# Clustered attention and a gated FFN on one core: one sum, one reciprocal and one product for the two heads of a pair in the first batch, with a new table of places

## Chip, cores and metric

The kernel runs on one core of a Trainium2 chip. The metric is the time of the device for one execution in microseconds (us). The engines are named as in the profile: PE (TensorE, matrix products; PEld is its weight load), ACT (ScalarE), DVE (VectorE), POOL (GpSimd) and SP (SyncE, which issues most DMAs).

## The reference

Attention in which a query sees only the keys of its own cluster, followed by a gated FFN. There are 4 batches, 8 heads, 768 positions and 64 dimensions for a head.

```python
q_assign = argmax(einsum('bhsd,hcd->bhsc', q_n, c_n))      # q_n, k_n, c_n: normalised; 16 clusters for a head
k_assign = argmax(einsum('bhsd,hcd->bhsc', k_n, c_n))
mask = q_assign[:, :, :, None] == k_assign[:, :, None, :]
scores = where(mask, (1 / 8) * q @ k.T, -1e9)
attn = softmax(scores) ; a = attn @ v                      # x: 3072 tokens x 512, heads side by side
gate = sigmoid(x @ w_gate) ; val = x @ w_val               # 512 -> 1536
out = (gate * val) @ w_out                                 # 1536 -> 512
```

## The kernel before

The work of a batch is cut into *steps*. One step takes 128 keys of one head and the queries of a half of the sequence (3 chunks of 128): PE makes the scores (`sc`, line 652), ACT takes the exponential into `es` (line 657), and three steps later PE multiplies `es` by the head's v with a column of ones beside it (`av`, line 675), so that the weighted sum and the sum of weights gather in one PSUM tile. In batch 0 all four pairs of heads are run half by half: steps 0 to 47 are the first half of the queries of heads 0 to 7 (six steps for a head, so head 7 begins at step 42), steps 48 to 95 the second half.

The mask is part of the product. Before a head's first step its k and q are split into two float16 parts: a high half (`hi`, a cast, line 873) and a low half (`lo`, the difference, line 880), laid side by side in `hl`. PE transposes `hl` into PSUM (`tu`, `t_ps`, line 901), and an engine copies that to `T` (`ev`, lines 912 and 914). PE multiplies `T` by the centroids (`lg`, line 390), DVE takes the maximum and compares (`pk`, lines 929 and 937), PE transposes the result (`ot`, `oh_ps`, line 961), and it is placed in rows 64 to 79 of `T` (`pl0` for k, line 982; `pl1` for q, line 986): two positions of different clusters then get a large negative score. The second half of a pair's queries, "the rest" (`r0` to `r3`, lines 997 to 1056), goes the same way later.

When a head's six steps are done, `normalise` (lines 335 to 347) adds to `av` a tiny multiple of the sum of v (`sv`), takes the reciprocal of the sum of weights, both on DVE (lines 339 and 341), and multiplies on POOL into one half of the pair's tile `xp` (line 344). After the pair's second head `xp` is transposed into `xT`, by PE (`x_ps`, line 703) and a copy (line 704) or by a DMA. The FFN of half a batch needs all four pairs of that half: `g` (line 477) and `v` (line 497) are its two first products, `o` (line 517) the last. They are put into a queue from which every step takes a few.

The order on each engine is written out by a table, `SCHED`. A place such as `"h4lo0": 5.0` says that this piece (head 4, low half, side 0 = k) is issued behind step 5; `r0hi` is the high half of pair 0's rest, `vc` the cast of v, `w` the weight loads, `b1p2tn0` a piece of batch 1, pair 2. Keys that end in `E` choose the engine (`A` ACT, `D` DVE, `P` POOL); without one, `hi`, `ev` and places are DVE's and `lo` POOL's. The engines run their queues in order, each as fast as its waits allow: places fix the order, not the time. `nd7` would put dummy products ahead of step 7's scores. The branch that the table now switches on is in the program already:

```python
both = nq == 3 and b < SCHED.get("pn", 0)
...
elif e == 1:
    normalise2(av, nq, b, p, x)
```

Of the kernel before, what the change touches and what calls it, by code (L numbers as in the profile page):

```python
# [19 lines left out]
]  # L20
SCHED = {
# [70 lines left out]
}  # L92


# [1254 lines left out]
```

## Time and profile before

| | |
|---|---|
| time, median of 3 runs | 327.67 us (327.52 to 328.28) |
| the profiled execution | 328.03 us, of which the span from the first to the last instruction is 325.9 us |
| granted TensorE clock | 1.000 |
| busy, share of the span | PE 98%, PEld 64%, DVE 59%, ACT 72%, POOL 33% |
| first score, first gate product | 9.09 us, 40.37 us |
| HBM | 28.34 MB read, 6.29 MB written |

A row of the timeline gives start, duration, engine, line, operation and output<-input, with the idle time before it and what ended it in brackets. A row of a group gives shapes, the count, the busy time, the mean duration of one in ns, and the idle time before them. Matmul records overlap: the distance from one start to the next is shorter than a record.

### The profile page before, as it was taken

What the parts mean: (1) busy time and instruction counts of PE and PEld (TensorE: products, weight loads), DVE (VectorE), ACT (ScalarE), POOL (GpSimd) and SP (SyncE); (2) the same over time, 40 slices, a digit from 0 to 9 for tenths busy, and PEclk for the clock granted to TensorE, in tenths of its full rate; (3) what the DMA queues carried; (4) which work ended last, traced back from release to release, by engine and by line L of the source; (5) the groups of instructions that cost most, each with busy time, mean ns of one, the idle gap of its engine ahead of it and who ended that gap; (6) DMA issues with size and microseconds to landing.
All of it is one profiled execution on the core that took longest, in us unless ns stands there. A gap on an engine that the chain in (4) does not pass through costs nothing.

```text
span 325.9 us, 8840 instructions
## 1 busy us (share of the span) xinstructions
PE 319.4 (98%) x3363; PEld 207.7 (64%) x3363; DVE 190.7 (59%) x527; ACT 234.8 (72%) x527; POOL 108.4 (33%) x150
## 2 busy tenths in 40 slices
PE   7999999999999999999999999999999999999996
PEld 5878766766766666666566655666566655654654
DVE  5899858877767666657546655667544322441431
ACT  6697998777899988877677777887778877332420
POOL 5876554143435365334232443323210111000000
PEclk9999999999999999999999999999999999999999
DMA  6999996719896995963897473932731012102002
GB/s 190 360 263 188 266 157 116 208 28 203 230 221 174 152 260 128 275 180 76 159 196 172 135 98 103 252 82 53 139 91 37 2 24 78 44 2 94 3 2 97
DMA packets 77994, 45.14 MB, mean 139 GB/s; under 512 B 56896, under 2 KB 75008, under 8 KB 77952
## 3 DMA queue, kind: packets, MB, share of 16 engines
q1 hardware_dynamic: 73984, 39.73, 51.5%
q0 software_dynamic: 3680, 4.72, 8.7%
q8 instruction: 26, 0.43, 0.5%
q14 instruction: 16, 0.13, 0.1%
q10 hardware_dynamic: 288, 0.13, 0.1%
HBM read 28.34 MB, written 6.29 MB: 106 GB/s over the span
## 4 chain that ended last, share of the span: by engine, by line
PE 92%; DVE 3%; DMA 2%; ACT 1%; POOL 1%; issue 1%; ACTq 0%; DVEq 0%
PE g L477 19%; PE v L497 19%; PE o L517 18%; PE sc L652 18%; PE av L675 10%; PE lg L403 2%; DMA kraw<-in_k_dram 2%; PE o_end L549 1%; PE lg L390 1%; PE t_ps L901 1%; PE wm L743 1%; DVE T L982 1%; PE oh_ps L961 1%; POOL hl L880 0%; PE t_ps L784 0%
## 5 line engine op out<-in xcount | busy, mean ns | idle before, releaser
L657 ACT ACTIVATE es<-sc 128x384 f16<-128x384 f32 x384 | 175.1, 493 | 42.6 <-PE sc L652 37.2
L652 PE MATMUL sc<-T 128*128 128x384 f16 x384 | 117.9, 326 | 0.7 <-DVE T L986 0.4
L675 PEld LDWEIGHTS <-es 128*128 128x128 f16 x1152 | 81.5, 98 | 49.1 <-ACT es L657 0.2
L675 PE MATMUL av<-va,es 128*128 128x65 f16 x1152 | 97.6, 194 | 0.0
L504 DVE SCALAR_TENSOR_TENSOR hT<-th,v 128x384 f16<-128x384 f32 x96 | 53.2, 554 | 67.1 <-PE av L675 44.7
L497 PE MATMUL v<-xTb,wv 128*128 128x384 f16 x384 | 78.1, 326 | 0.0
L477 PE MATMUL g<-xTb,wg 128*128 128x384 f16 x384 | 78.0, 326 | 0.0
L517 PE MATMUL o<-wo,hT 128*128 128x512 f16 x276 | 75.1, 379 | 0.0
L344 POOL TENSOR_TENSOR xp<-t,rec 128x192 f16<-128x192 f32 (+1 forms) x46 | 29.6, 643 | 126.9 <-DVE rec L341 76.1
L485 ACT ACTIVATE th<-g 128x384 f32<-128x384 f32 x96 | 47.2, 492 | 25.6 <-DVE hT L504 17.9
L477 PEld LDWEIGHTS <-wg 128*128 128x128 f16 x384 | 37.2, 97 | 20.4
L497 PEld LDWEIGHTS <-wv 128*128 128x128 f16 x384 | 37.4, 98 | 19.9
L652 PEld LDWEIGHTS <-T 128*128 128x128 f16 x384 | 37.1, 97 | 1.1 <-DVE T L986 1.1
L517 PEld LDWEIGHTS <-hT 128*128 128x128 f16 x276 | 26.7, 97 | 16.2
L339 DVE TENSOR_TENSOR t<-av,sv 128x195 f32<-128x195 f32 (+1 forms) x46 | 20.1, 437 | 24.4 <-PE av L675 20.8
L1215 POOL TENSOR_TENSOR hl<-kraw,hl 128x384 f16<-128x384 f32 x22 | 20.7, 945 | 24.3 <-issue 13.6
L1215 POOL TENSOR_TENSOR hl<-qraw,hl 128x384 f16<-128x384 f32 x22 | 21.6, 983 | 12.2 <-DVE hl L1214 11.2
L418 DVE TENSOR_REDUCE lgs<-lg 128x192 f32<-128x384 f32 x23 | 12.7, 551 | 11.4 <-PE lg L403 11.3
L526 ACT ACTIVATE ob<-o 128x512 f32<-128x512 f32 x15 | 8.9, 595 | 10.8 <-PE o L517 10.7
L291 POOL CAST va<-vraw 128x768 f16<-128x768 f32 x16 | 13.5, 842 | 2.5 <-DMA vraw<-in_v_dram 2.5
L524 DVE TENSOR_SCALAR ob<-o 128x512 f32<-128x512 f32 x8 | 5.5, 691 | 13.6 <-PE o L517 13.4
L403 PE MATMUL lg<-cm,T 128*128 128x32 f16 x288 | 11.1, 176 | 0.0
(115 smaller groups left out, 232.3 us busy)
## 6 DMA issues: line engine op xcount, KB each, us to landing
vraw<-in_v_dram SPq DMA_DIRECT2D x16, 384.0 KB, 5.5
out_dram<-ob SPq DMA_DIRECT2D x23, 256.0 KB, 2.2
kraw<-in_k_dram SPq DMA_DIRECT2D x15, 384.0 KB, 5.1
qraw<-in_q_dram SPq DMA_DIRECT2D x12, 384.0 KB, 4.9
wg<-in_moe_w_gate_dram POOLq DMA_DIRECT2D x2, 768.0 KB, 9.2
wv<-in_moe_w_val_dram POOLq DMA_DIRECT2D x2, 768.0 KB, 8.9
wo<-in_moe_w_out_dram POOLq DMA_DIRECT2D x2, 768.0 KB, 8.8
qraw<-in_q_dram SPq DMA_DIRECT2D x7, 192.0 KB, 6.7
```

The source lines that it names most:

```text
L339: DVE.tensor_tensor(t[:, 0:nq, :], av, sv, ALU.add)
L344: (eng or POOL).tensor_tensor(x, t[:, 0:nq, 0:64], bcast(rec[:, 0:nq], 64), ALU.mult)
L403: PE.matmul(out=lg[:, bass.ts(i, 32)], lhsT=t[:, c, :], rhs=cm[:, h].rearrange("p s n -> p (s n)"), start=True, stop=True,)
L477: PE.matmul(out=g[:, 0:n], lhsT=wg[fc // WQ][:, dc, fc % WQ, :], rhs=xT[:, dc, t0 : t0 + n], start=(dc == 0), stop=(dc == NDC - 1),)
L485: ACT.activation(th[:, 0:n], g[:, 0:n], AF.Tanh, scale=0.5)
L497: PE.matmul(out=w[:, 0:n], lhsT=wv[fc // WQ][:, dc, fc % WQ, :], rhs=xT[:, dc, t0 : t0 + n], start=(dc == 0), stop=(dc == NDC - 1),)
L504: DVE.scalar_tensor_tensor(hT[:, fc, 0:n], st[1][:, 0:n], 1.0, w[:, 0:n], ALU.add, ALU.mult)
L517: PE.matmul(out=o, lhsT=hT[:, fc, bass.ts(t, 128)], rhs=wo[fc // WON][:, fc % WON, :], start=(fc == 0), stop=(fc == NFC - 1),)
L652: PE.matmul(out=sc.rearrange("p (c t) -> p c t", t=128), lhsT=s["k"], rhs=s["q"], start=True, stop=True,)
L657: ACT.activation(es, sc, AF.Exp, scale=SCALE)
L675: PE.matmul(out=av[:, a0 + s["c0"] + i, :], lhsT=s["es"][:, bass.ts(i, 128)], rhs=VA[b, p][:, e, s["j"], :], start=(first and i == 0 and a ...
L1215: POOL.tensor_tensor(hl[:, :, 64:128], r, hl[:, :, 0:64], ALU.subtract)
```

## The change

The key `pn` is set to 1. For batch 0 (in both halves, since each takes three chunks) the two heads of a pair now share one PSUM tile of 6 x 65 columns; nothing is normalised behind the first head, and behind the second head `normalise2` does the addition, the reciprocal and the product for both. On DVE that is 16 instructions fewer in the program (465 to 449), on POOL 8 products fewer. Apart from this, the table is redone: some 130 places move, most by half a step or one step; a few pieces change engine; three dummy products of 128 columns are put ahead of steps 7, 8 and 46; the loads of batch 0 are issued in another order; and the sum of v of the last pair uses another PSUM pool. Several new keys (`lq`, `lp`, `cd`, `tx`) are read nowhere in this program. The core of the diff, by keys:

```diff
+"pn": 1
-"h4hi0": 1.0, "h4lo0": 5.0, "h5lo0": 8.5, "h6lo0": 23.5
+"h4hi0": 2.0, "h4lo0": 4.5, "h5lo0": 7.5, "h6lo0": 20.5
-"h3lg": 10.5, "h3pk": 11.0, "h4pl0": 20.0, "h4pl1": 22.0, "h7pl0": 40.0, "h7pl1": 40.5
+"h3lg": 9.0, "h3pk": 10.0, "h4pl0": 21.5, "h4pl1": 20.5, "h7pl0": 40.0, "h7pl1": 39.5
-"r0hiE": "A", "h4ev1E": "A", "h5ev1E": "A"            (now DVE)
-"h6lo1E": "D", "r3loE": "D"                           (now POOL)
+"h7hi0E": "P", "r0ev1E": "A", "g0pl1E": "A"           (were DVE)
-"w00": 2.5, "r1tu": 46.5, "r1ot": 54.5, "lag01": 5.5
+"w00": 4.5, "r1tu": 45.5, "r1ot": 53.5, "lag01": 4.5
+"nd7": 1, "nd8": 1, "nd46": 1
-loads of batch 0:  v0 k1 q1 v1 k2 q2 v2 k3 q3 v3
+loads of batch 0:  v0 k1 q1 k2 q2 v1 v2 q3 k3 v3
+"vso33": 1
```

```python
def normalise2(av, nq, b, p, x):
    t = tmpp.tile([128, NCH, 65], FP, name="t")
    sv = SV[b, p].unsqueeze(2).to_broadcast([128, 2, nq, 65])
    DVE.tensor_tensor(t (2, nq, 65), av (2, nq, 65), sv, ALU.add)
    rec = smp.tile([128, NCH], FP, name="rec")
    DVE.reciprocal(rec, t[:, :, 64:65])
    POOL.tensor_tensor(x (nq, 2, 64), t[:, :, 0:64], bcast(rec, 64), ALU.mult)
```

133 rows, old and new, of the table SCHED are left out of this document.

## The prediction

> **What bounds the kernel now.** I read the busy time by stretches first, then the chain of waits, then the waits of the stretch in which PE is not full.
>
> ```profile
> 10.00:20.00 10.00, 9.41 (x172) 7.78 (x169) 8.50 (x28) 8.06 (x20) 9.14 (x15) 1.00 1.09 343
> 20.00:30.00 10.00, 9.48 (x179) 7.78 (x177) 9.54 (x30) 8.11 (x22) 7.38 (x12) 1.00 1.09 188
> 30.00:40.00 10.00, 9.62 (x177) 7.73 (x174) 8.36 (x29) 9.01 (x25) 5.38 (x9) 1.00 1.09 263
> 40.00:50.00 10.00, 10.00 (x106) 6.71 (x103) 5.79 (x16) 8.98 (x23) 5.79 (x9) 1.00 0.98 166
> ...
> 280.00:300.00 20.00, 20.00 (x113) 10.89 (x112) 6.17 (x11) 5.63 (x12) 0.00 (x0) 1.00 0.07 27
> ```
>
> The columns behind the length are PE, PEld, DVE, ACT, POOL, the clock, DMA share and GB/s. From 40 us on PE is busy in the whole of every stretch (the last row shows a late one); before that it is not, and there DVE (9.54 of 10 us between 20 and 30) and POOL (9.14 between 10 and 20) are as full as PE. Busy PE time overstates PE, because the records of consecutive matmuls overlap. The chain of waits shows the true pace:
>
> ```profile
> 40.53 0.65 PE g L477 x4
> ...
> 291.53 7.77 PE o L517 x36
> ```
>
> Four matmuls of 384 columns take 0.65 us (0.16 each, where one record lasts 0.33), and 36 of 512 columns 7.77 us (0.216 each). From the first gate product at 40.4 us to the end PE is a single queue of such work, which the edit neither adds to nor takes from. So the whole effect must come from when this queue starts, which is decided before 40 us. How much is there to win? The waits between 9 and 42 us (waiter, releaser, us in total, times, longest):
>
> ```profile
> PEld L901 <- POOL hl L880: 1.2, 3, 0.5
> PEld L652 <- DVE T L986: 1.1, 3, 0.5
> ...
> PEld L961 <- issue: 0.4, 2, 0.2
> PEld L703 <- POOL xp L344: 0.2, 1, 0.2
> ```
>
> The weight load stands ahead of its matmul and is short, so its waits are PE's real pauses: 1.2 us for the low halves that POOL subtracts, 1.1 for the last place that DVE writes into a head's T, 0.4 + 0.2 for smaller ones. Together 2.9 us: more than this cannot be won without changing the lead-in, whose orders are the same in both programs up to the third score. The largest single pause, with the load's engine, and what follows it on ACT:
>
> ```profile
> 34.30 0.36 DVE L986 TENSOR_SCALAR T<-oh_ps 16x384 f16<-16x384 f16 x1
> 34.72 0.34 PE L652 MATMUL sc<-T 128*128 128x384 f16 x1 [0.38 <-DVE T L986]
> ...
> 35.09 6.24 ACT L657 ACTIVATE es<-sc 128x384 f16<-128x384 f32 x16 [0.31 <-PE sc L652]
> ```
>
> Step 42, the first of head 7, starts when DVE has placed its mask rows (34.66). After it ACT runs 16 exponentials without a pause, 0.39 us each, up to 41.33. So an earlier place of head 7 moves the start of those 16, and with it the gate product, by as much.
>
> **The joint normalisation.** It holds for both halves of batch 0, since every pair there runs three chunks at a time: eight pairs, of which three (pairs 0 to 2) end before step 42.
>
> ```profile
> L339 DVE TENSOR_TENSOR t<-av,sv 128x390 f32<-128x390 f32 x18 | 10.1, 561 | 6.3 <-PE av L675 6.3
> L339 DVE TENSOR_TENSOR t<-av,sv 128x195 f32<-128x195 f32 x16 | 5.7, 359 | 16.8 <-PE av L675 13.9 <-issue 2.0 <-POOL hl L1215 1.0
> L341 DVE RECIPROCAL rec<-t 128x6 f32<-128x6 f32 x18 | 3.5, 193 | 0.6
> L341 DVE RECIPROCAL rec<-t 128x3 f32<-128x3 f32 x16 | 2.8, 176 | 0.6
> ...
> L344 POOL TENSOR_TENSOR xp<-t,rec 128x384 f16<-128x384 f32 x18 | 15.3, 848 | 80.2 <-DVE rec L341 38.7 <-issue 36.7 <-PE v L497 4.7
> L344 POOL TENSOR_TENSOR xp<-t,rec 128x192 f16<-128x192 f32 x28 | 14.3, 511 | 46.7 <-DVE rec L341 37.4 <-issue 7.2 <-DMA T<-ohT 1.3
> ```
>
> These rows are of the stretch behind 57 us (DVE) and of the whole run (POOL): the later batches already run the wide shape, so its price is known. DVE: 2 x (0.359 + 0.176) - (0.561 + 0.193) = 0.32 us less for a pair, 0.95 for three. POOL: 2 x 0.511 - 0.848 = 0.17 less, 0.52 for three.
>
> **Work moved between engines before step 42.** To DVE from ACT: the high half of pair 0's second part and the second T copies of heads 4 and 5. From DVE to POOL: the low half of head 6's q and the high half of head 7's k. From DVE to ACT: one copy of pair 0's second part.
>
> ```profile
> L914 DVE COPY T<-t_ps 128x384 f16<-128x384 f16 x3 | 1.1, 351 | 0.0
> L880 DVE TENSOR_TENSOR hl<-qraw,hl 128x192 f16<-128x192 f32 x5 | 3.0, 592 | 0.0
> L873 DVE CAST hl<-kraw 128x384 f16<-128x384 f32 x4 | 1.7, 425 | 0.0
> L880 POOL TENSOR_TENSOR hl<-qraw,hl 128x192 f16<-128x192 f32 x3 | 1.7, 554 | 1.1 <-DVE hl L873 1.0
> L873 POOL CAST hl<-kraw 128x384 f16<-128x384 f32 x2 | 1.1, 567 | 0.0
> L912 ACT COPY T<-t_ps 128x384 f16<-128x384 f16 x7 | 3.2, 477 | 0.9 <-PE t_ps L901 0.9
> ```
>
> DVE: + 3 x 0.35 - 0.59 - 0.43 - 0.35 = - 0.32. With the normalisation DVE has 1.27 us less to do before head 7's place. POOL: + 0.55 + 0.57 - 0.52 = + 0.6. ACT: three for one, some 0.95 less; it waits for scores there (the 0.31 in its row), so that is worth nothing by itself.
>
> What DVE saves it may lose by a lock:
>
> ```profile
> 12.04 0.92 POOL L880 TENSOR_TENSOR hl<-kraw,hl 128x384 f16<-128x384 f32 x1
> 12.51 0.67 DVE L880 TENSOR_TENSOR hl<-qraw,hl 128x192 f16<-128x192 f32 x1
> ```
>
> The DVE operation, 0.35 us when alone, ends at 13.18, 0.22 behind the end of POOL's (12.96): it lay still while POOL ran. So each DVE operation that reads raw data from SBUF costs up to 0.3 to 0.4 more behind a POOL one. The high half that DVE takes over is such an operation, among POOL's low halves: I charge 0.3 for it and take DVE's gain at head 7's place as 1.27 - 0.3 = 0.97 us, between 0.27 (two more of them locked, at 0.35 each) and 1.27 (no new lock). The Trainium skill's SBUF — State Buffer, Who interferes with whom, says that a DVE instruction with two SBUF inputs and a GpSimd one that reads SBUF exclude each other, and that the later one blocks fully: the trace agrees (0.67 for 0.35). Taken at its strictest, with the trace's 0.92 for the lock in place of my 0.3, it would leave the sum below at + 0.1 us, an estimate from that page.
>
> **Places redone.** Pair 2's k and q are loaded ahead of pair 1's v, and the low half of head 4's k goes on POOL ahead of the weight load:
>
> ```profile
> 4.12 0.47 SPq L192 DMA_DIRECT2D vraw<-in_v_dram  x1
> ...
> DMA to landing us min/median/max: 6.8/6.8/6.8
> ...
> 13.49 0.83 POOL L291 CAST va<-vraw 128x768 f16<-128x768 f32 x1
> ...
> 14.26 0.94 POOL L234 DMA_DIRECT2D wg<-in_moe_w_gate_dram  x1
> ...
> 16.28 0.91 POOL L880 TENSOR_TENSOR hl<-kraw,hl 128x384 f16<-128x384 f32 x1
> ...
> 17.25 0.51 PE L901 MATMUL t_ps<-identh,hl 128*128 128x128 f16 x6 [0.34 <-POOL hl L880]
> ```
>
> (The first two rows are the load of pair 1's v and its time to land.) From 14.26 to 16.28 POOL does that issue, a v cast and a q cast; without them ahead, the low half ends near 15.2 instead of 17.19, and the pause of 0.5 at 17.25 (0.34 and the 0.16 by which records overlap) goes. What is late next is DVE's place of head 3, so this gain is the same time as DVE's and isn't counted twice. The queues that it is moved past: gate weights are issued some 2 us later, with 24 us until the first gate product reads them; v of pair 1 landed at 10.9 and is now issued behind two more loads (576 KB, 1.7 us at the 343 GB/s of the row of 10 to 20 us), so it lands at 12.6, ahead of its cast (13.49). Both: nothing. Head 6's low half of k likewise moves up.
>
> **The pair that closes the first half.** Here the wide shape costs, for nothing else is left to hide it:
>
> ```profile
> 38.04 0.36 DVE L339 TENSOR_TENSOR t<-av,sv 128x195 f32<-128x195 f32 x1
> 38.44 0.18 DVE L341 RECIPROCAL rec<-t 128x3 f32<-128x3 f32 x1
> ...
> 38.69 0.51 POOL L344 TENSOR_TENSOR xp<-t,rec 128x192 f16<-128x192 f32 x1 [1.26 <-DVE rec L341]
> ...
> 39.26 0.34 PE L703 MATMUL x_ps<-identh,xp 128*128 128x128 f16 x3
> ...
> 40.37 0.81 PE L477 MATMUL g<-xTb,wg 128*128 128x384 f16 x4
> ```
>
> Sum, reciprocal, product and transpose follow each other; only the second head's part stood in this chain before. It grows by (0.56 - 0.36) + 0.02 + (0.85 - 0.51) = 0.56 us. PE's queue waits at the transpose; behind it stand a weighted sum, three scores and the gate product. The mask transposes of the rest, three of 0.057 (six take 0.34 in the chain), are moved ahead of it and fill 0.17. Loss 0.39, between 0 (if PE too comes to it later than now) and 0.56.
>
> **Dummy matmuls.** Three of 128 columns, ahead of steps 7, 8 and 46: 3 x 0.057 = 0.17 if PE is full there, nothing in a pause. I take 0.05.
>
> **Behind 40 us.** Order changes by one place here and there, with DVE at 5.8 of 10 us: 0, between - 0.4 and + 0.4. The second half's joint normalisation lies beside the first half's FFN.
>
> **Sum.** - 0.97 + 0.39 + 0.05 = - 0.53 us; with the bounds of the terms, from - 1.7 to + 0.9. The profiled execution took 328.03 us, 2.1 more than its span; it would take 327.5. The median of the runs is 327.67, 0.36 less, so I predict 327.1 us. The measurement tells 0.3% (1.0 us) from no change, so this is no change, if barely.
>
> **Rivals.**
> *All pauses go.* Moves of POOL's low halves and of DVE's places work together: of the 2.9 us the first pause stays, and 2.3 of the rest go, less 0.44 for the closing pair and the dummies: - 1.9, 325.8 us.
>
> ```profile
> 11.85 0.23 PE L901 MATMUL t_ps<-identh,hl 128*128 128x128 f16 x1 [0.24 <-POOL hl L880]
> ```
>
> (The first pause, 0.24 + 0.16, before any difference in order.) For it: DVE's 1.27 less, and the two POOL pauses of heads 4 and 6 both addressed. Against: DVE and PE are both at 9.5 of 10, and a pause that goes on one brings the other to the front.
>
> *POOL becomes the bound.* It has 9.14 of 10 us between 10 and 20 and gets 0.6 more by 30; its queue is in order, so a joint product that waits for DVE's reciprocal holds the casts and low halves of heads 6 and 7 behind it. Then the transposes of these heads come 0.6 later than now, DVE's casts are locked for two more low halves (+ 0.7), and the closing chain costs its full 0.56 with the dummies' 0.17: 0.6 + 0.7 + 0.56 + 0.17 - 0.97 = + 1.06, 328.7 us. It decides from the point where the low half of head 6's k ends later than it does now. Against: the moved weight issue gives POOL back 0.94 at the right place.
>
> *Hidden.* ACT's 16 exponentials or PE's order set the gate product whatever head 7 does: 0 to + 0.3, 327.8 us. Against: ACT waited 0.31 for step 42.
>
> **Numbers.** Forecast 0.37, all pauses go 0.34, hidden 0.12, POOL 0.17. Faster by over 0.3% is the second, 0.34; within it the first and the third, 0.49; slower 0.17. The range reaches to 325.8, the second rival's price, and to 328.4, most of the way to POOL's: about one case in ten lies beyond either end.
>
> **What would show it.** Right: weight loads L652 wait less than 0.7 us for DVE's places, the waits for POOL at L901 fall to the first one, head 7's first score stands near 33.8 and the first gate product near 39.8, and a pause of some 0.3 appears ahead of the closing transpose. Wrong: a first gate product that moved by over 1 us either way, a new pause behind 40 us, or DVE casts of 0.6 us and more throughout.

## The result, and the profile after

| | before | after |
|---|---|---|
| time, median | 327.54 us (22 runs) | 326.71 us (22 runs, 326.06 to 328.22) |
| ratio, 95% interval | | 0.9974 [0.9966, 0.9983] |
| profiled execution, span | 328.03 us, 325.9 us | 328.22 us, 326.4 us |
| second score, first gate product | 11.28 us, 40.37 us | 10.71 us, 39.28 us |

The change takes 0.83 us off, with an interval of 0.56 to 1.11 (the ratio times 327.54): within 0.3%, where the forecast stood, with 0.4 us between the forecast time (327.1) and the measured one. One run of before took 411.75 us, a slow one that the ratio leaves out. The profiled execution of after is its slowest: it holds a pause of 1.5 us at 120.5 us that a second profile of the same program, the first experiment, does not have.

Line numbers of after lie 3 above those of before (scores L655, low halves' transposes L904, closing transpose L706). The busy time by stretches of after, with the columns of the prediction's table:

```profile
10.00:20.00 10.00, 9.55 (x183) 8.00 (x184) 8.75 (x28) 8.07 (x19) 9.17 (x15) 1.00 1.09 342
20.00:30.00 10.00, 9.76 (x181) 8.26 (x179) 9.61 (x29) 8.25 (x20) 9.02 (x15) 1.00 1.06 182
```

PE is fuller between 10 and 30 us (9.55 and 9.76 for 9.41 and 9.48). DVE is about as full as before there (8.75 and 9.61 for 8.50 and 9.54), though it has less to do for the same work: the same time now holds more of it. POOL, which took over two pieces, is fuller between 20 and 30 us (9.02 for 7.38). Of the waits of 9 to 42 us in after (us in total, times, longest), the three largest of PE's weight loads:

```profile
PEld L904 <- POOL hl L883: 0.9, 2, 0.5
PEld L655 <- DVE T L985: 0.7, 2, 0.5
...
PEld L964 <- issue: 0.5, 2, 0.4
```

In before POOL's low halves cost 1.2 and DVE's places 1.1. The low half of head 4's k moved up as foreseen, and nothing waits for it (timeline of after):

```profile
13.81 0.92 POOL L883 TENSOR_TENSOR hl<-kraw,hl 128x384 f16<-128x384 f32 x1
...
14.96 0.94 POOL L237 DMA_DIRECT2D wg<-in_moe_w_gate_dram  x1
...
16.87 0.50 PE L904 MATMUL t_ps<-identh,hl 128*128 128x128 f16 x6
```

It ended at 17.19 and now ends at 14.73, and the transposes have no idle time ahead of them. But step 42 still waits for head 7's place (timeline of after):

```profile
31.49 0.56 DVE L354 TENSOR_TENSOR t<-av,sv 128x390 f32<-128x390 f32 x1
...
32.09 0.19 DVE L359 RECIPROCAL rec<-t 128x6 f32<-128x6 f32 x1
32.31 0.36 DVE L989 TENSOR_SCALAR T<-oh_ps 16x384 f16<-16x384 f16 x1
...
32.68 0.56 DVE L985 COPY T<-oh_ps 16x768 f16<-16x768 f16 x1
...
33.30 0.34 PE L655 MATMUL sc<-T 128*128 128x384 f16 x1 [0.37 <-DVE T L985]
```

From one matmul start to the next, PE loses 0.54 us here, as much as before. Directly ahead of head 7's two places DVE now has the joint sum and reciprocal of pair 2 (31.49 to 32.28). In before, head 5's own sum and reciprocal stood in that place (timeline of before):

```profile
33.12 0.35 DVE L339 TENSOR_TENSOR t<-av,sv 128x195 f32<-128x195 f32 x1
...
33.51 0.18 DVE L341 RECIPROCAL rec<-t 128x3 f32<-128x3 f32 x1
```

They are 0.53 us of work, and the joint ones 0.75: 0.22 more at this place.

The closing pair (timeline of after):

```profile
36.59 0.56 DVE L354 TENSOR_TENSOR t<-av,sv 128x390 f32<-128x390 f32 x1 [0.36 <-PE av L678]
...
37.18 0.19 DVE L359 RECIPROCAL rec<-t 128x6 f32<-128x6 f32 x1
...
37.46 0.82 POOL L360 TENSOR_TENSOR xp<-t,rec 128x384 f16<-128x384 f32 x1 [3.83 <-DVE rec L359]
...
38.34 0.17 PEld L706 LDWEIGHTS <-xp 128*128 128x128 f16 x3 [0.28 <-POOL xp L360]
```

The pause of 0.28 ahead of the closing transpose is the one that the prediction announced.

**A measure by parts.** To see where each kernel below gains or loses, I took from each profile the starts of five matmuls: the second score (step 1), the scores of steps 12 and 42, the first gate product, and the last matmul, which starts 3.4 us ahead of the end of the span in every one. All in us; the first column is the median of the runs.

| kernel | time | step 12 behind the second score | 12 to 42 | 42 to gate product | gate product to last matmul |
|---|---|---|---|---|---|
| before | 327.54 | 7.18 | 16.26 | 5.64 | 282.14 |
| after | 326.71 | 6.92 | 15.66 | 5.99 | 283.76 |
| after_again | 326.81 | 6.78 | 15.58 | 5.98 | 282.24 |
| pn_only | 329.52 | 7.13 | 16.29 | 6.15 | 283.60 |
| places_only | 328.48 | 6.93 | 16.05 | 5.84 | 283.42 |
| closing_split | 326.63 | 6.91 | 15.67 | 5.77 | 282.12 |
| late_norm2 | 326.39 | 6.92 | 15.42 | 6.20 | 282.11 |
| late_norm | 327.01 | 6.76 | 15.62 | 6.20 | 282.11 |
| late_norm3 | 326.26 | 6.75 | 15.28 | 5.82 | 282.12 |
| old_engines | 327.94 | 6.92 | 16.65 | 5.98 | 282.61 |
| act_copies | 327.86 | 6.91 | 16.58 | 5.98 | 282.42 |
| dve_halves | 327.41 | 6.91 | 16.28 | 5.99 | 282.11 |
| no_dummies | 326.90 | 6.86 | 15.69 | 5.93 | 282.12 |
| old_loads | 326.89 | 6.91 | 15.66 | 5.99 | 282.12 |

What lies ahead of the second score is left out of it: its place varies by execution (10.71 and 11.03 us for the same program), see the last section.

### The profile page after: what moved, and what is told of

It is laid out like the page before. It is cut to its first block, busy times and chain, and to the rows that moved or that the text cites. A ratio compares the mean times of both kernels' runs of the same rounds, so it can differ in the third digit from the quotient of the medians.

```text
span 326.4 us, 8811 instructions
## 1 busy us (share of the span) xinstructions
PE 318.0 (97%) x3366; PEld 205.8 (63%) x3366; DVE 187.4 (57%) x509; ACT 235.6 (72%) x526; POOL 108.4 (33%) x145
## 3 DMA queue, kind: packets, MB, share of 16 engines
HBM read 28.34 MB, written 6.29 MB: 106 GB/s over the span
## 4 chain that ended last, share of the span: by engine, by line
PE 86%; DMA 4%; POOL 3%; DVE 3%; issue 2%; SPq 1%; ACT 0%; POOLq 0%
PE g L480 19%; PE v L500 19%; PE o L520 17%; PE sc L655 16%; PE av L678 9%; DMA T<-hl 2%; PE lg L406 2%; DMA kraw<-in_k_dram 2%; PE o_end L552 1%; POOL xp L360 1%; POOL hl L883 1%; POOL hl L1004 1%; PE t_ps L904 0%; PE lg L393 0%; PE t_ps L787 0%
## 5 line engine op out<-in xcount | busy, mean ns | idle before, releaser
L655 PE MATMUL sc<-T 128*128 128x384 f16 x384 | 118.0, 325 | 0.7 <-DVE T L985 0.4
L347 POOL TENSOR_TENSOR xp<-t,rec 128x384 f16<-128x384 f32 (+1 forms) x30 | 21.2, 705 | 107.8 <-DVE rec L344 56.4
L655 PEld LDWEIGHTS <-T 128*128 128x128 f16 x384 | 37.1, 97 | 1.2 <-DVE T L985 0.7
L342 DVE TENSOR_TENSOR t<-av,sv 128x390 f32<-128x390 f32 (+1 forms) x30 | 14.4, 480 | 20.5 <-PE av L678 16.2
```

Source lines behind the costliest of these rows:

```text
L342: DVE.tensor_tensor(t[:, 0:nq, :], av, sv, ALU.add)
L347: (eng or POOL).tensor_tensor(x, t[:, 0:nq, 0:64], bcast(rec[:, 0:nq], 64), ALU.mult)
L655: PE.matmul(out=sc.rearrange("p (c t) -> p c t", t=128), lhsT=s["k"], rhs=s["q"], start=True, stop=True,)
```

## The experiments

**The same program again: after_again.**

```diff
+ # the same program
```

> The changed kernel once more, for a second profile. Its first profile has a pause of 1.5 us at 120.5 us (logits of batch 2 wait for a DMA transpose) and a first gate product at 39.28 us. Theory A (the gain is made before the first gate product, by DVE's relief and POOL's new order): first gate product near 39.3 to 39.9 again, 0.5 to 1.1 us ahead of the 40.37 of before; time 326.7. Theory B (the 0.6 us by which its first score came earlier, 8.36 for 9.09, made the gain, and that is chance): the distance from the second score to the first gate product is that of before, 29.1 us, and not 28.6. On the pause: if it belongs to the kernel, it is there again at 1 us or more and the time is near 328; if it belongs to one execution, it is gone.

Measured: 326.81 us (12 runs), ratio 0.9979 [0.9970, 0.9989]. Where the first profile had a pause at 120.5 us this one has none. The logits of a later head in after (PE), and in the second profile (PE):

```profile
122.07 0.47 PE L406 MATMUL lg<-cm,T 128*128 128x32 f16 x12 [1.35 <-DMA T<-hl]
```

```profile
120.66 0.45 PE L406 MATMUL lg<-cm,T 128*128 128x32 f16 x12
```

They wait for a DMA transpose of `hl` that SP issues in both (timeline of after, SP; the second has it at 114.98, 1.53 us long):

```profile
114.88 2.46 SPq L382 DMA_TRANSPOSE T<-hl  x1
```

In the first it landed 7.1 us behind its issue, and the product that waited started at 7.2; in the second it landed after 3.8 us, and PE, which came to it 5.7 us behind the issue, had no wait. So this pause is chance in one execution and no part of the change's time. Theory B falls: the first score of the second profile stands at 9.06 us, as late as in before, and the distance from the second score to the first gate product is still 28.34 us, for 29.08 in before. From the second score to the last matmul the second profile is 0.64 us shorter than before (- 0.40, - 0.68, + 0.34, + 0.10 by the columns), beside 0.70 in the medians (326.81 for 327.51 on this chip).

**The joint normalisation alone, on the old places: pn_only.**

```diff
+"pn": 1                      # all else as before
```

> The kernel before with the joint normalisation alone (all places as before). Theory A: DVE has 0.95 us less before step 42, the closing pair costs 0.39: second score to first gate product 28.4 to 28.9 us (before 29.1), time 327.0 to 327.4. Rival C (the places and the engine moves make the gain, the joint form by itself only lengthens the chain of each pair): 29.1 to 29.5 us, time 327.6 to 328.1.

Measured: 329.52 us (5 runs, 328.97 to 329.71), ratio 1.0058 [1.0046, 1.0070]: 2.0 us slower than before, and outside of what the theories gave. Two things lose. First, head 7's place comes no sooner behind the second score, because the joint sum of pair 2 stands directly ahead of it, where head 5's shorter one stood (timeline of pn_only):

```profile
32.54 0.55 DVE L352 TENSOR_TENSOR t<-av,sv 128x390 f32<-128x390 f32 x1
...
33.13 0.19 DVE L357 RECIPROCAL rec<-t 128x6 f32<-128x6 f32 x1
...
33.94 0.36 DVE L987 TENSOR_SCALAR T<-oh_ps 16x384 f16<-16x384 f16 x1
...
34.36 0.34 PE L653 MATMUL sc<-T 128*128 128x384 f16 x1 [0.60 <-DVE T L987]
```

Behind the second score pn_only is 0.33 us ahead of before at step 24 and 0.23 at step 36, and at step 42 only 0.02: the idle time of PE ahead of that score is 0.60 for 0.38, longer by the 0.22 that the joint sum and reciprocal are longer than head 5's own. So of the 0.95 us of work that DVE saves over three pairs hardly anything arrives at step 42, and steps 12 to 42 take 16.29 us for 16.26. Then the closing pair costs 0.51 (6.15 for 5.64). Second, there is a loss behind 57 us that no theory had (waits of PE's weight loads in pn_only):

```profile
PEld L404 <- DMA T<-hl: 1.2, 1, 1.2
```

That is a pause at 87.3 us, for a DMA transpose again. It landed 4.1 us behind its issue (3.8 in before), but SP issued it 1.2 us later than in before (84.49 for 83.31). SP's queue, which runs in order, stood ahead of it for 3.7 us until another DMA transpose, `ohT<-oh`, had landed; in before it was 2.7 (6.6 for 5.6 us from issue to landing). Why that one landed later stays open. All five runs take 328.97 us or more, so unlike after's pause this one seems to belong to the program; no second profile was taken to show it. 0.49 up to the gate product and 1.46 behind it make 1.95 of the 2.01 us.

**The new places alone: places_only.**

```diff
-"pn": 1
+"pn": 0                      # all else as after
```

> The changed kernel with the normalisation by heads again (new table, engines, loads and dummies kept). Theory A: DVE has 0.95 us more before step 42 and the closing pair's 0.28 pause goes: second score to first gate product 28.9 to 29.4 us, time 327.0 to 327.5. Rival C: the gain stays and the closing loss goes: 28.2 to 28.6 us, time 326.3 to 326.7.

Measured: 328.48 us (5 runs), ratio 1.0033 [1.0020, 1.0046]: 1.0 us slower than before, and outside of what the theories gave. Up to the gate product it is 0.26 better than before (0.25 + 0.21 - 0.20), and behind it 1.28 worse (waits of PE's weight loads from 40 to 70 us, then the timeline of the first of them):

```profile
PEld L481 <- issue: 0.5, 1, 0.5
PEld L656 <- DVE T L990: 0.4, 1, 0.4
PEld L840 <- DVE oh L819: 0.4, 1, 0.4
```

```profile
47.42 0.91 POOL L1219 TENSOR_TENSOR hl<-qraw,hl 128x384 f16<-128x384 f32 x1 [0.29 <-DVE hl L1218]
...
47.53 0.91 DVE L1042 TENSOR_TENSOR oh<-lgs,mx 128x96 f16<-128x96 f32 x1
...
48.37 0.34 DVE L708 COPY xTb<-x_ps 128x384 f16<-128x384 f16 x1
...
48.77 0.81 PE L481 MATMUL g<-xTb,wg 128*128 128x384 f16 x4 [0.27 <-DVE xTb L708]
```

The compare takes 0.91 us where the same line, with the same shape and inputs, takes 0.26 at 56.84 us: it starts 0.11 behind POOL's low half and ends 0.11 behind it. The copy of the FFN's input waits behind the compare, and PE for the copy. Of the other two waits the last is for a compare again (0.49 us at 62.44, beside a product of POOL); the one for a place, at 53.09, was not followed. So the two halves of the change are no sum: + 2.0 and + 1.0 apart, - 0.8 together. Up to the gate product alone it is + 0.49 and - 0.26 apart and - 0.51 to - 0.74 together.

This run also isolates the joint sum at head 7's place, for here head 5's own stands there (timeline of places_only):

```profile
34.05 0.34 PE L656 MATMUL sc<-T 128*128 128x384 f16 x1 [0.15 <-DVE T L986]
```

The idle time is 0.15 for 0.37 in after: the same 0.22 as between before (0.38) and pn_only (0.60). So the new places shorten this pause by 0.23, and the joint sum puts 0.22 back.

**The closing pair of the first half head by head: closing_split.**

```diff
-both = nq == 3 and b < SCHED.get("pn", 0)
+both = nq == 3 and b < SCHED.get("pn", 0) and not (p == 3 and s["h1"] == 0)
```

> The changed kernel, only that the last pair of the first half is normalised head by head. Theory A: the pause of 0.28 us ahead of the closing transpose goes and nothing takes its place: first gate product 0.2 to 0.3 us earlier, time 326.4 to 326.5. Rival D (ACT's row of exponentials sets the gate product, and PE meets the same wait one step later): 0 to 0.1 us, time 326.7.

Measured: 326.63 us (11 runs), ratio 0.9976 [0.9967, 0.9984]. Step 42 to the gate product takes 5.77 for 5.98: 0.21 of the 0.34 comes back. The other 0.13 is no matter of the width of the sum and product, and was not traced. The medians differ by 0.18, which the intervals don't resolve by themselves.

**Pair 2's joint sum behind head 7's place (with the closing pair split): late_norm2.**

```diff
+"nz20": 2.25, "xt20": 10.5      # issue it 2.25 steps later, its transpose later too
+late = SCHED.get(f"nz{p}{s['h1']}", 0) if both else 0
-normalise2(av, nq, b, p, x)
+at(step_no[0] + late, lambda: normalise2(av, nq, b, p, x))
```

> The changed kernel with the closing pair head by head, and pair 2's joint sum, reciprocal and product issued behind head 7's places on DVE instead of ahead of them (its transpose 4 steps later). Theory A (DVE's queue ahead of head 7's place sets step 42): 0.56 + 0.19 us leave that queue, the 0.54 pause ahead of step 42 goes, second score to first gate product 27.8 to 28.0 us (closing_split 28.35), time 326.1 to 326.2. Rival D (ACT's row of exponentials or PE's order sets the gate product): the pause goes, the gate product does not move: 28.2 to 28.4, time 326.6.

Measured: 326.39 us (8 runs), ratio 0.9958 [0.9942, 0.9975]. The pause at step 42 is halved (0.54 to 0.29), but a new one of 0.39 stands ahead of the mask transposes of pair 0's rest, whose compare is now what the joint sum stands ahead of (timeline of late_norm2):

```profile
33.01 0.57 DVE L355 TENSOR_TENSOR t<-av,sv 128x390 f32<-128x390 f32 x1
...
33.61 0.19 DVE L360 RECIPROCAL rec<-t 128x6 f32<-128x6 f32 x1
...
33.97 0.26 DVE L1046 TENSOR_TENSOR oh<-lg,mx 128x96 f16<-128x96 f32 x1
...
34.28 0.34 PE L1064 MATMUL oh_ps<-identh,oh 128*128 128x128 f16 x3 [0.22 <-DVE oh L1046]
```

Against closing_split this gives 12 to 42 a gain of 0.25 in the trace and loses 0.43 behind it. From the second score to the gate product it is 28.54 us, which neither theory gave. The median is lower all the same (326.39 for 326.63), so the time alone can't decide this one.

**The same for pair 0 too: late_norm.**

```diff
+"nz00": 3.25, "xt00": 10.5      # beside the edit above
```

> As late_norm2, and pair 0's joint sum, reciprocal and product behind head 3's places too. Theory A: the 0.3 pause ahead of step 18 goes as well: step 18 stands 0.2 to 0.3 us nearer to the second score, and 0.1 to 0.3 of it reaches the first gate product: 27.6 to 27.9 us, time 325.9 to 326.1. Rival E (DVE is full, so what is taken from one head's queue is paid in the next's): step 18 earlier, step 24 and all behind it as in late_norm2.

Measured: 327.01 us (12 runs), ratio 0.9979 [0.9965, 0.9994]. Step 18 comes 0.22 to 0.44 us earlier than in after's two profiles (9.41 us behind the second score, for 9.63 and 9.85) and step 24 is back between them (12.72, for 12.58 and 12.81), for head 5's compare, which comes next on DVE, is late instead (timeline of late_norm):

```profile
20.81 0.56 DVE L355 TENSOR_TENSOR t<-av,sv 128x390 f32<-128x390 f32 x1
...
21.82 0.37 DVE L945 TENSOR_TENSOR oh<-lg,mx 128x96 f16<-128x96 f32 x2
...
22.25 0.51 PE L969 MATMUL oh_ps<-identh,oh 128*128 128x128 f16 x6 [0.66 <-DVE oh L945]
```

DVE is full here: what is taken from one head's queue is paid by the next, as rival E had it.

**The old engines of the moved pieces, on the new places: old_engines.**

```diff
-"h7hi0E": "P", "r0ev1E": "A"
+"h4ev1E": "A", "h5ev1E": "A", "r0hiE": "A", "h6lo1E": "D"
```

> The changed kernel with the six pieces ahead of step 42 on the engines that they had (high half of pair 0's rest and second copies of heads 4 and 5 on ACT; low half of head 6's q, high half of head 7's k and second copy of pair 0's rest on DVE). Theory A: DVE has 0.3 us more and one to two locked operations more: step 42 0.3 to 0.6 us later, second score to first gate product 28.7 to 29.0 us, time 327.0 to 327.3. Rival F (POOL, which gets 1.1 us less here, was the bound): 28.0 to 28.3 us, time 326.4 to 326.6.

Measured: 327.94 us (12 runs), ratio 1.0011 [0.9996, 1.0026]: the whole gain goes, more than either theory gave. Steps 12 to 42 take 16.65 us, 1.0 more than in after, with one pause of 1.09 us that begins near 18.7. The two parts were separated next.

**Only the three pieces that went from ACT to DVE, put back on ACT: act_copies.**

```diff
+"h4ev1E": "A", "h5ev1E": "A", "r0hiE": "A"
```

> The changed kernel with only the three pieces back on ACT (high half of pair 0's rest, second T copies of heads 4 and 5). Theory H (old_engines lost its 1 us because ACT's copy of head 4, behind five exponentials in ACT's queue, keeps a PSUM buffer that PE's next transposes need): the pause of 1.1 us near 18.7 us is there again, second score to first gate product 29.2 to 29.6 us, time 327.6 to 328.0. Theory A (DVE's load alone decides; here it has 1 us less): 27.8 to 28.3 us, time 326.2 to 326.6.

Measured: 327.86 us (12 runs), ratio 1.0011 [0.9999, 1.0023]; from the second score to the gate product 29.47 us, 0.9 to 1.1 more than after's two profiles (28.57 and 28.34). This alone is as much as the old engines together. The timeline of act_copies:

```profile
17.58 0.33 PE L905 MATMUL t_ps<-identh,hl 128*128 128x128 f16 x3
...
18.50 0.50 ACT L1001 CAST hl<-qraw 128x384 f16<-128x384 f32 x1
18.90 0.87 ACT L661 ACTIVATE es<-sc 128x384 f16<-128x384 f32 x2
...
19.65 0.49 ACT L916 COPY T<-t_ps 128x384 f16<-128x384 f16 x1
...
20.19 0.49 PE L905 MATMUL t_ps<-identh,hl 128*128 128x128 f16 x6 [0.93 <-ACT T L916]
```

The second T copy of head 4 stands in ACT's queue behind the cast of the rest and two exponentials, and begins 1.7 us behind the end of the transposes that it reads (17.91). Until it is done its PSUM tile isn't free, and PE's next six transposes wait 0.93 us for it. So theory H stands: in the new order ACT holds the PSUM tile. In the old order it doesn't: in before the same copy is ACT's too (19.21 us, 0.6 behind the end of its transposes), and PE's next six transposes, at 20.24, have no wait; the new table has this copy two steps later in the order (`h4ev1` 13.5 for 11.5).

**Only the other three pieces put back, from POOL and ACT to DVE: dve_halves.**

```diff
-"h7hi0E": "P", "r0ev1E": "A"
+"h6lo1E": "D"
```

> The changed kernel with only the three pieces back on DVE (low half of head 6's q, high half of head 7's k, second copy of pair 0's rest). Theory A: DVE has 1.4 us more, partly in its own waits: step 42 0.5 to 1.2 us later, second score to first gate product 28.9 to 29.5 us, time 327.2 to 328. Theory H: these pieces hold no buffer that PE waits for: 28.3 to 28.6 us, time 326.7 to 327.0.

Measured: 327.41 us (12 runs), ratio 0.9992 [0.9980, 1.0004]. Steps 12 to 42 take 16.28 us, 0.6 to 0.7 more than after, with pauses of 0.54 at step 18 and 0.48 at step 42. The prediction took 0.59 + 0.43 + 0.35 = 1.37 us off DVE for these three; about half of that is seen in the time of these steps. Act_copies lost 1.0 and dve_halves 0.65, and both at once (old_engines) 1.0: these are no sum either.

**No dummies: no_dummies.**

```diff
-"nd7": 1, "nd8": 1, "nd46": 1
+"nd7": 0, "nd8": 0, "nd46": 0
```

> The changed kernel without the three dummy products ahead of steps 7, 8 and 46. Theory A: 3 x 0.056 us of PE where it has little slack: 0 to 0.15 us sooner. Rival G (they hold PE at its fast pace in the early steps): a longer distance of matmul starts (107 for 56 ns at 128 columns) somewhere before step 42, and 0.3 us or more lost.

Measured: 326.90 us (11 runs), ratio 0.9971 [0.9958, 0.9985], 28.48 us from the second score to the gate product: no difference from after that the time or the trace resolves.

**The loads in the old order: old_loads.**

```diff
-loads of batch 0:  v0 k1 q1 k2 q2 v1 v2 q3 k3 v3
+loads of batch 0:  v0 k1 q1 v1 k2 q2 v2 k3 q3 v3
```

> The changed kernel with the loads of batch 0 issued in the order of before (pair 1's v ahead of pair 2's k and q). By the first prediction the loads are worth nothing: second score to first gate product 28.3 to 28.6 us, time 326.7 to 326.9. Rival: pair 2's k, which now lands 1 us later, holds POOL's cast of head 4 and with it the transposes near 16 us: 28.7 to 29.2 us, time 327.0 to 327.5.

Measured: 326.89 us (11 runs), ratio 0.9981 [0.9966, 0.9996]; 12 to 42 takes 15.66 us, as in after to the hundredth. The order of the loads does nothing that the time or the trace resolves.

**Pair 2's joint sum behind head 7's place and behind the compare: late_norm3.**

```diff
-"nz20": 2.25
+"nz20": 2.75                    # else as in late_norm2
```

> As late_norm2, but pair 2's joint sum also stands behind the compare of pair 0's rest on DVE, so that neither head 7's places nor that compare waits for it. Theory A': in late_norm2 the pause ahead of step 42 only moved to the transposes of that compare (0.39 us); with both ahead of the sum, both pauses shrink: step 42 at 22.2 to 22.4 us behind the second score, the gate product at 27.9 to 28.2 (closing_split 28.35), time 326.2 to 326.5. Rival D (ACT's row of exponentials and PE's order set the gate product): step 42 as in late_norm2, gate product 28.3 to 28.6, time 326.6.

Measured: 326.26 us (7 runs, 326.14 to 326.46), ratio 0.9958 [0.9943, 0.9974], the lowest median of all. The timeline of late_norm3:

```profile
32.38 0.56 DVE L990 COPY T<-oh_ps 16x768 f16<-16x768 f16 x1
...
32.98 0.10 PEld L656 LDWEIGHTS <-T 128*128 128x128 f16 x1 [0.24 <-DVE T L990]
...
33.26 0.26 DVE L1046 TENSOR_TENSOR oh<-lg,mx 128x96 f16<-128x96 f32 x1
33.43 0.55 DVE L355 TENSOR_TENSOR t<-av,sv 128x390 f32<-128x390 f32 x1
...
33.86 0.33 PE L1064 MATMUL oh_ps<-identh,oh 128*128 128x128 f16 x3
```

The weight load of step 42 waits 0.24 for 0.49, and the mask transposes not at all, since the sum is now the last of the three on DVE. The second score to the gate product takes 27.85 us, 0.49 to 0.72 less than in after's two profiles, and the median lies 0.45 below after's. It is faster than before by 1.26 us on the same chip; against after, the two intervals overlap, and it is the trace that shows the gain.

## Why the prediction was right, and where it was not

**The size and its sign.** Forecast - 0.53, measured - 0.83, with the forecast just outside of the interval (0.56 to 1.11). Of the table's columns, step 42 behind the second score was forecast 0.97 earlier: it is 0.86 and 1.08 in the two profiles of after. Step 42 to the gate product was forecast 0.39 longer: 0.35 and 0.34. Behind the gate product 0 was forecast, and the profile without the chance pause has + 0.10. The dummies (0.05) and the loads (0) can't be told from nothing. The wide operations cost what the later batches said: the joint product was priced at 848 ns and is 825 (groups of the first 57 us of after):

```profile
L360 POOL TENSOR_TENSOR xp<-t,rec 128x384 f16<-128x384 f32 x6 | 5.0, 825 | 6.3 <-DVE rec L359 6.3
```

**What was to be seen.** The pause of 0.3 ahead of the closing transpose, the place of head 7's score (33.8; 33.30 and 33.40) and of the gate product (39.8; 39.28 and 39.38) came out, the last two half a microsecond early. The waits for DVE's places were to be less than 0.7: they are 0.7. Of the waits for POOL only the first was to stay: 1.2 became 0.9, for a new one of 0.35 ends at head 3's transposes, at 12.44 us. The second profile doesn't have it, and there 0.3 is left. And a gate product that moved by over 1 us was to show the forecast wrong: it moved by 1.09 and 0.99. In the first profile 0.57 of that lies ahead of the second score, where the prediction saw the same orders; the steps themselves hold the 0.51 and 0.74 that are left, 0.02 under and 0.21 over the sum.

**The route to step 42 was another.** The prediction put DVE's gain at head 7's place. The pause there stayed at 0.54, for the joint sum put back what the new places took off, and the gain came from earlier pauses: 0.51 at head 4's transposes, 0.26 at step 24 and 0.30 at head 6's transposes are gone, with 0.14 at step 39 new. The joint sum of three pairs had been counted as less work for DVE; that the piece which stands directly ahead of head 7's place grows by 0.22 had not. In pn_only hardly anything of the 0.95 arrived at step 42, and late_norm3 takes out half the pause.

**The sum was right partly by luck.** Its terms can be held against the table, by how much later step 42 comes, behind the second score, when one piece of the change is undone. After's two profiles have it at 22.58 and 22.36 us. Without the joint form (places_only) it is 22.98: 0.40 to 0.62, where 0.95 was counted. With the three pieces back on DVE (dve_halves) it is 23.19: 0.61 to 0.83, where 1.37 was counted. With the three pieces back on ACT (act_copies) it is 23.49: 0.91 to 1.13, where their move to DVE was counted as a loss of 1.05 and 0.3 more for the lock. So two terms were about twice too large and one had the wrong sign, and that their sum of 0.97 came out beside 0.86 and 1.08 is in part luck. These are prices for one piece at a time in the new order, and they add up to more than the whole.

**The lock.** 0.3 was charged for the cast that DVE took over. Its row among the groups of the first 57 us of after:

```profile
L1000 DVE CAST hl<-qraw 128x384 f16<-128x384 f32 x1 | 0.3, 350 | 0.0
```

350 ns is what DVE's free copies of that shape took before, so the charge wasn't due. That holds for this place: another cast of that shape on DVE, at 21.90 us in after, takes 0.62 and ends 0.22 behind a low half of POOL, as one took 0.67 in before. The lock at its plainest is in places_only: 0.91 us for 0.26. The rule of the Trainium skill's SBUF — State Buffer, Who interferes with whom, that the later of two such instructions waits for the whole of the earlier, agrees with this row. A locked compare need not cost time: in after the same one takes 0.70 at 46.60 us, and PE has no wait there.

**ACT's relief: the step that failed.** "Worth nothing by itself" was priced from the row of 16 exponentials at the end, where ACT waits for scores. But at 17 to 20 us ACT runs without a pause, and in the new order a copy behind the exponentials holds a PSUM tile: act_copies puts 0.9 to 1.1 us on it, more than the whole effect. The price was taken from another stage than the one in which the piece stands. In the old order it was worth nothing indeed, for PE had no wait for this copy there: the new order needs the relief.

**Behind 40 us.** 0 holds for the change as a whole, but not for its parts (+ 1.46 and + 1.28). That DVE is busy for only 5.8 of 10 us there did not protect against a lock or a DMA transpose at the wrong moment.

**The rivals.** *POOL becomes the bound* named its own point: the low half of head 6's k ending later than it does. It ended at 25.56 and now starts at 22.66 and ends at 23.57, 2 us earlier, since it now stands ahead of a low half of a q, a product and a q cast that POOL did before it. *Hidden* is refuted by late_norm3: a step 42 that is 0.33 to 0.55 earlier than in after has a gate product 0.49 to 0.72 earlier (some 0.2 of it by the split closing pair), so the gate product follows step 42 there. It need not: in late_norm2 step 42 came 0.24 earlier than in closing_split and the gate product 0.19 later, by the new pause behind it. *All pauses go*: of its 2.3 us, 1.0 went (0.86 to 1.08). PE's own pauses at steps 18, 42 and the closing transpose (0.30, 0.54, 0.28) are the main part of what is left of it, and the prediction's reason against it, that with DVE and PE both at 9.5 of 10 a pause that goes brings another, is what late_norm shows.

## What to carry to other kernels

When two small operations become one wide one, ask not only what it saves but where the one piece lands: work that was spread comes as a lump in front of whatever is next in the queue, and it can pay to move it behind the next items that another engine waits for (late_norm3), though on a full engine this may only move the pause (late_norm). A copy out of PSUM is priced by the queue that it stands in, not by its length: on an engine that runs without a pause it can hold the tile, and the engine that wants to write it, for as long as that queue is. A change to a written-out order can't be judged by its parts, since each part alone may lose what the whole gains.

## What was not expected of the hardware

**The start varies by execution.** The first score and the three transposes behind it, PE in before and then in after:

```profile
9.09 0.53 PE L652 MATMUL sc<-T 128*128 128x384 f16 x1
9.41 0.53 PE L901 MATMUL t_ps<-identh,hl 128*128 128x128 f16 x3
```

```profile
8.36 0.34 PE L655 MATMUL sc<-T 128*128 128x384 f16 x1 [0.21 <-DVE T L989]
8.53 0.33 PE L904 MATMUL t_ps<-identh,hl 128*128 128x128 f16 x3
```

384 columns take 0.32 us from start to start in the first and 0.17 in the second, though the column of the granted clock reads 1.00 in both. The second profile of after has the slow pace at this place too (0.53 us at 9.06). So it is no effect of the change. Between the two profiles of after the first score stands 0.7 us apart and the second 0.3. The Trainium skill's TensorE: Matmul & The Clock Gate, Part 1: The HAM clock gate, says that the array starts at half pace, and that the window which ends this runs free of the kernel's start; the rows, half the pace in one execution and the full one in the other, are in keeping with it, and no run here shows the window itself.

**DMA transposes land late now and then.** The DMA issues of after (count, median us from issue to landing):

```profile
T<-hl SPq DMA_TRANSPOSE x24, 4.2
```

One of these 24 landed 7.1 us behind its issue in this execution, and after 3.8 us in the other profile of the same program, where PE came to what it brings 5.7 us behind the issue. So a chain that passes through one can have a pause in one execution and none in the next (1.5 us in after). The pause of 1.2 us in pn_only is another case: its transpose landed as fast as in before and was issued 1.2 us later.
